# Swapping two of the small products of a split matmul, and drawing both score products of a block together, in a linear-attention and Mish kernel

## The chip, the cores and the metric

The kernel runs on one core of a Trainium2 chip. The metric is device time in microseconds (us) of one execution; lower is better. The median of three runs of the kernel before is 208.18 us (207.81 to 208.47).

## The reference, cut to what matters

```python
# retention: B=4, H=8, S=768, D=64
state = gamma[None, :, None, None] * state + einsum('bhd,bhe->bhde', k[:, :, t], v[:, :, t])
y[:, :, t] = scale * einsum('bhd,bhde->bhe', q[:, :, t], state)     # for every t
x = y.transpose(0, 2, 1, 3).reshape(B * S, H * D)                   # 3072 x 512
h = x @ w_in                                                        # 512 -> 2048
g = h * tanh(softplus(h))                                           # Mish
out = g @ w_out                                                     # 2048 -> 512
```

## The kernel before, in words

The 3072 tokens are 24 chunks of 128, grouped in 11 blocks: one of four chunks, then ten of two (256 tokens). A block goes through retention (scores, mask, outer product, state, y), then through the first product with Mish (`g1`), then through the second product (`g2`). TensorE ("PE") does all products in fp16. The retention work of the following block is woven by hand into the products of the current one: the schedule is manual, so every engine runs its instructions in the order in which the Python text issues them.

From block 3 (`SEVEN`) on, so in the last eight blocks, half of `g1` and all of `g2` are done as a 2x2 split with seven small products instead of eight, the sums and differences of the operands being made on VectorE ("DVE"). `g1_seven` writes the split half of `g1` into three PSUM tiles: `pb`, `px`, `pe`. `mm` is one small product, 8 matmuls of 128 columns. `px` is used four times: its contents after the first and after the third use are copied out by ScalarE ("ACT") with `snap` (L606, as `m1` and `u2`); `pe` is copied once (`m5`). `plus` (L616) is a DVE addition of a PSUM tile and such a copy, and gives `c11`, `c12`, `c22`; `mish_of` (L610) is the Mish of such a quarter on ACT. The other half of `g1` is done in four whole units, `plain(1,0)`, `plain(1,1)`, `plain(3,0)`, `plain(3,1)`: 8 matmuls of 256 columns each (L623) and one Mish on ACT (L627). A product that accumulates on a PSUM tile must wait until earlier readers of that tile are through.

Where `g1_seven` calls `step(name)`, the woven work of `steps_of` is issued. `scores(g)` (L371) makes the scores of chunk `g`: 8 matmuls with weights of 64 rows and 128 columns, into a tile of the pool `atps`, which has two buffers shared by the outer products `u_ps`, both score tiles and `y_ps`. `mask(g)` (L377) multiplies them by the causal mask on DVE. With `a = first[blk] + 4`, chunks `a - 2` and `a - 1` belong to the next block; the last block has no such work.

`sums_a(blk, half)` (L543 and L544, a pair of DVE operations) makes half of the operands `s1` and `s2` of the second product out of `g`. Half 0 needs the Mish of `c11`, `c12` and `c22`; half 1 needs the Mish of all four plain units. `seven` then does the second product: `mm(px, a(0,0))`, `mm(pb, a(0,1))`, `mm(px, s(2))` and so on (L688), 8 matmuls of 256 columns each. The third of these takes its weights from `s2`: its first four matmuls from half 0, its last four from half 1.

GpSimd ("POOL") casts the loaded q, k and v (L319, L324, L325) and finishes the states (L398). SyncE ("SP") issues loads, stores and the transposes of q and k by DMA (L331).

The end of `g1_seven`, around the change, reads:

```python
step("p6")
plain(1, 0)
mm(pe, s(4), b(1, 1));  c12 = plus(pe, u2)
mm(px, s(3), t(3));     c22 = plus(px, m5)
mish_of(0, 1, c12);     mish_of(1, 1, c22)
step("p7")              # stores, second state, sums_a half 0
plain(1, 1)
mm(px, a(1, 1), t(4));  mish_of(1, 0, px)
step("p4")              # stores, scores(a - 2), mask(a - 2)
plain(3, 0);  plain(3, 1)
step("end")             # sums_a half 1, scores(a - 1), casts, loads
```

Of the kernel before, what the change touches and what calls it, by code (L numbers as in the profile page):

```python
# [16 lines left out]
def kernel(  # L17
# [78 lines left out]
    for c in range(2):  # L96
        t = tri_first[c * HB:(c + 1) * HB]
# [367 lines left out]
    def win(s, f, bp):  # L465
        return wins[s, f // 2][:, bp, f % 2 * P:(f % 2 + 1) * P]
# [13 lines left out]
    def xt(blk, bp):  # L480
        return xts[0][:, :, bp] if blk == 0 else xts[blk][:, bp, :BLOCKS[blk] * C]
# [82 lines left out]
    def x_part(blk, i, j):  # L564
        n = NBP // 2
        return xts[blk][:, i * n:(i + 1) * n, j * P:(j + 1) * P]
# [10 lines left out]
    def g1_seven(blk, steps):  # L577
        n = NBP // 2
        gt = gtiles[blk, 0] = gp.tile([P, NFB, 2 * P], FP16, name="g", tag="g")
        for fb in range(NFB):  # L580
            gts[blk, fb] = gt[:, fb]
        pb, px, pe = [mmps.tile([P, FPS, P], FP32, name="h_ps", tag="mm") for _ in range(3)]

        def a(i, j):
            return lambda f, d: win(2 * i, f, j * n + d)

        def s(i):
            return lambda f, d: wsums[0][:, i - 1, d, f * P:(f + 1) * P]

        def b(i, j):  # L590
            return lambda d: x_part(blk, i, j)[:, d]

        def t(i):
            return lambda d: tsums[blk][:, i - 1, d]

        def mm(h_ps, w, x, first=False):
            for f in range(FPS):
                for d in range(n):
                    nc.tensor.matmul(  # L599
                        h_ps[:, f], w(f, d), x(d), start=first and f == 0 and d == 0,  # L600
                        stop=d == n - 1, skip_group_check=True)

        def snap(h_ps):
            x = hsnaps[0][:, nsnap[0] % 4].rearrange("p (f t) -> p f t", t=P)
            nsnap[0] += 1
            nc.scalar.copy(x, h_ps)  # L606
            return x

        def mish_of(i, j, h):
            nc.scalar.activation(  # L610
                gt[:, 2 * i * FPS:(2 * i + 1) * FPS, j * P:(j + 1) * P], h, AF.Mish,
                scale=inv_boost3)

        def plus(h_ps, x):
            h = hp.tile([P, FPS, P], FP32, name="hsum", tag="hsum", bufs=3)
            nc.vector.tensor_tensor(h, h_ps, x, op=ALU.add)  # L616
            return h

        def plain(s, half):
            h_ps = mmps.tile([P, 2, 2 * P], FP32, name="h_ps", tag="mm")  # L620
            for j in range(2):
                for bp in range(NBP):
                    nc.tensor.matmul(  # L623
                        h_ps[:, j], win(s, 2 * half + j, bp), xt(blk, bp),
                        start=bp == 0, stop=bp == NBP - 1)
            fb = s * FPS + 2 * half
            nc.scalar.activation(gt[:, fb:fb + 2], h_ps, AF.Mish, scale=inv_boost3)  # L627

        def step(name):
            for fn, *args in steps.get(name, ()):  # L630
                fn(*args)

        mm(px, a(0, 0), b(0, 0), True)
        m1 = snap(px)
        mm(pb, a(0, 1), b(1, 0), True)
        c11 = plus(pb, m1)
        step("p2")
        mm(pe, s(1), t(1), True)
        m5 = snap(pe)
        mm(px, s(2), t(2))  # L640
        u2 = snap(px)
        mish_of(0, 0, c11)
        step("p6")
        plain(1, 0)
        mm(pe, s(4), b(1, 1))
        c12 = plus(pe, u2)
        mm(px, s(3), t(3))
        c22 = plus(px, m5)
        mish_of(0, 1, c12)
        mish_of(1, 1, c22)  # L650
        step("p7")
        plain(1, 1)
        mm(px, a(1, 1), t(4))
        mish_of(1, 0, px)
        step("p4")
        plain(3, 0)
        plain(3, 1)
        step("end")

# [227 lines left out]
    def steps_of(blk):  # L887
        a, nb = first[blk] + 4, blk + 1
        ahead = nb < len(BLOCKS)

        def only(*work):
            return list(work) if ahead else []
        return {
            "p2": only((outer_next, nb), (state_next, nb, 0)),
            "p6": [(cast_to, a + 1), (next_chunk, a), (store_due, 1)],
            "p7": [(store_due, 2), *only((state_next, nb, 1)), (sums_a, blk, 0)],
            "p4": [(store_due, 3), *only((scores, a - 2), (mask, a - 2))],
            "end": [(sums_a, blk, 1), *only((scores, a - 1)),
                    (cast_to, a + 2), (next_chunk, a + 1)],
            "m2": only((mask, a - 1)),  # L900
            "m7": only((y_two, nb)),
            "m3": only((x_sums, nb)),
        }
# [13 lines left out]
    for blk in range(1, len(BLOCKS)):  # L917
        if blk >= SEVEN:
            steps = steps_of(blk)
            g1_seven(blk, steps)  # L920
            seven(blk, steps, blk + 1 == len(BLOCKS))
            continue
# [7 lines left out]
        for u in range(2 * n1):  # L930
# [3 lines left out]
            else:  # L934
                t, part = divmod(u - n1, 4)
# [43 lines left out]
```

## Time and profile before

| | |
|---|---|
| median of three runs | 208.18 us (207.81 to 208.47) |
| profiled execution | 207.9 us, of which the span of instructions is 206.0 us |
| granted TensorE clock | 1.0 |
| PE busy | 197.2 us (96% of the span) |
| DVE, ACT, POOL busy | 143.1, 98.3, 90.6 us |
| one of the last eight blocks | 15.2 to 15.5 us |

In the views of the profile a row is an engine, a line of the kernel, the operation, and the tiles written and read. Times run from the start of the span. The chain of waits follows the work that ended last back to what released it; the timeline merges instructions that follow each other, so that a merged PE row ends with the modelled end of its last matmul while the next row has already begun. The distance between the starts of two PE rows is the time that the first one takes from TensorE.

### The profile page before, as it was taken

The page shows a single profiled execution, that of the slowest core. Times are in us where ns is not written, and L with a number is a line of the kernel's source. Part 1 is how long each engine was busy: PE and PEld are TensorE (multiplying, and loading weights), DVE is VectorE, ACT ScalarE, POOL GpSimd, SP SyncE. Part 2 cuts the span into 40 slices and gives each one's busy share as a digit, 9 for nine tenths or more (in the row PEclk, how much of TensorE's full clock was granted, in tenths as well). Part 3 has the DMA queues.
Part 4 walks back from the last instruction along what each step waited for, and adds up shares of the span by engine and source line. Part 5 has one row for each costly group of instructions (what it writes and reads, how often), then busy time and mean ns, then how long its engine had stood idle before and what let it go on. Part 6 is the DMA issues. An engine that isn't in the chain of part 4 may idle for free.

```text
span 206.0 us, 5180 instructions
## 1 busy us (share of the span) xinstructions
PE 197.2 (96%) x2167; PEld 150.2 (73%) x2167; DVE 143.1 (69%) x234; ACT 98.3 (48%) x171; POOL 90.6 (44%) x83
## 2 busy tenths in 40 slices
PE   6788999999999999999999999999999999999993
PEld 2355444456855865988988988888888888888882
DVE  2796644169937986788897787686897687686542
ACT  2462763242611621653653653753753743843840
POOL 4162000519955760399182594598091693200000
PEclk9999999999999999999999999999999999999999
DMA  5999999998999999939998159959999062200202
GB/s 177 299 316 363 386 387 279 292 220 176 201 247 262 216 221 237 180 70 214 227 253 178 35 109 225 178 105 267 194 256 190 18 156 56 100 0 26 80 28 77
DMA packets 95896, 38.64 MB, mean 188 GB/s; under 512 B 82305, under 2 KB 89985, under 8 KB 95873
## 3 DMA queue, kind: packets, MB, share of 16 engines
q1 hardware_dynamic: 92608, 37.50, 80.3%
q10 hardware_dynamic: 3264, 0.82, 2.4%
q8 instruction: 17, 0.28, 0.5%
q14 instruction: 7, 0.05, 0.1%
HBM read 27.30 MB, written 6.29 MB: 163 GB/s over the span
## 4 chain that ended last, share of the span: by engine, by line
PE 83%; DVE 9%; ACT 2%; DMA 2%; issue 2%; DVEq 0%
PE o_ps L688 24%; PE h_ps L475 13%; PE o_ps L497 11%; PE h_ps L599 11%; PE h_ps L623 11%; DVE hsum L616 5%; PE at L371 3%; PE y_ps L414 2%; DMA qfirst<-in_q_dram 2%; PE y_ps L404 2%; PE u_ps L385 2%; DVE am L377 1%; PE h_ps L760 1%; ACT xt L460 1%; DVE qfirst L196 1%
## 5 line engine op out<-in xcount | busy, mean ns | idle before, releaser
L319 POOL TENSOR_TENSOR qk<-qf,qvs 128x512 f16<-128x512 f32 x20 | 22.5, 1127 | 28.4 <-DMA qf<-in_q_dram 26.4
L623 PE MATMUL h_ps<-xt,win 128*128 128x256 f16 x256 | 31.9, 273 | 0.0
L398 POOL TENSOR_TENSOR st<-su,gcm 128x512 f16<-128x512 f32 x9 | 11.9, 1321 | 41.7 <-DVE su L397 31.3
L497 PE MATMUL o_ps<-wout,g 128*128 128x512 f16 x128 | 30.1, 380 | 0.0
L324 POOL TENSOR_SCALAR qk<-kf 128x512 f16<-128x512 f32 x18 | 27.8, 1546 | 2.1 <-DMA kf<-in_k_dram 0.6
L377 DVE TENSOR_TENSOR am<-at,tri 128x1024 f16<-128x1024 f32 x20 | 24.1, 1214 | 4.6 <-PE at L371 4.6
L688 PEld LDWEIGHTS <-gsum 128*128 128x128 f16 x256 | 24.4, 98 | 3.6 <-DVE gsum L666 0.2
L475 PE MATMUL h_ps<-xt,win 128*128 128x256 f16 (+1 forms) x184 | 26.5, 305 | 0.3
L623 PEld LDWEIGHTS <-win 128*128 128x128 f16 x256 | 23.7, 98 | 3.1
L475 PEld LDWEIGHTS <-win 128*128 128x128 f16 x184 | 18.0, 98 | 9.0 <-issue 0.8
L491 ACT ACTIVATE g<-h_ps 128x512 f16<-128x512 f32 x32 | 19.0, 597 | 11.4 <-PE h_ps L475 10.0
L325 POOL TENSOR_TENSOR v<-vf,qvs 128x512 f16<-128x512 f32 x20 | 21.6, 1079 | 6.3 <-DMA vf<-in_v_dram 4.9
L460 ACT CAST xt<-y_ps 128x1024 f16<-128x1024 f32 x10 | 10.1, 1012 | 28.9 <-PE y_ps L414 21.6
L616 DVE TENSOR_TENSOR hsum<-h_ps,hsnap 128x512 f32<-128x512 f32 x24 | 15.8, 686 | 9.4 <-PE h_ps L599 8.2
L688 PE MATMUL o_ps<-tmat,gsum 128*128 128x256 f16 x192 | 22.3, 273 | 0.0
L627 ACT ACTIVATE g<-h_ps 128x512 f16<-128x512 f32 x32 | 19.0, 593 | 4.8 <-PE h_ps L623 4.8
L497 PEld LDWEIGHTS <-g 128*128 128x128 f16 x128 | 11.7, 98 | 13.0 <-issue 0.3
L606 ACT COPY hsnap<-h_ps 128x512 f32<-128x512 f32 x24 | 13.3, 588 | 15.6 <-PE h_ps L599 15.6
L688 PEld LDWEIGHTS <-g 128*128 128x128 f16 x192 | 18.2, 98 | 2.8
L694 ACT COPY snap<-o_ps 128x256 f32<-128x256 f32 x24 | 8.9, 372 | 20.3 <-PE o_ps L688 20.3
L702 DVE TENSOR_TENSOR osb<-o_ps,snap 128x256 f32<-128x256 f32 x24 | 10.1, 419 | 11.7 <-PE o_ps L688 9.0
L610 ACT ACTIVATE g<-hsum 128x512 f16<-128x512 f32 x24 | 15.0, 635 | 3.4 <-DVE hsum L616 3.4
(94 smaller groups left out, 291.0 us busy)
## 6 DMA issues: line engine op xcount, KB each, us to landing
kf<-in_k_dram SPq DMA_DIRECT2D x23, 256.0 KB, 5.1
vf<-in_v_dram SPq DMA_DIRECT2D x23, 256.0 KB, 5.1
out_dram<-osb SPq DMA_DIRECT2D x22, 256.0 KB, 3.8
qf<-in_q_dram SPq DMA_DIRECT2D x19, 256.0 KB, 4.0
wt<-in_moe_w_out_dram SPq DMA_DIRECT2D x3, 1024.0 KB, 8.9
wi<-in_moe_w_in_dram SPq DMA_DIRECT2D x4, 512.0 KB, 7.3
wi<-in_moe_w_in_dram SPq DMA_DIRECT2D x2, 1024.0 KB, 11.3
qfirst<-in_q_dram SPq DMA_DIRECT2D x2, 512.0 KB, 5.0
```

What stands on the lines that cost most here:

```text
L319: nc.gpsimd.tensor_tensor(q16, qf, qs.unsqueeze(2).broadcast_to((P, H, D)), op=ALU.mult)
L324: nc.gpsimd.tensor_scalar(k16, kf, BOOST, None, op0=ALU.mult)
L325: nc.gpsimd.tensor_tensor(v16, vf, vs.unsqueeze(2).broadcast_to((P, H, D)), op=ALU.mult)
L377: nc.vector.tensor_tensor(am, ats.pop(g), tri.unsqueeze(1).unsqueeze(1).broadcast_to((P, 2, HP, C)), op=ALU.mult)
L475: nc.tensor.matmul(h_ps[:, j], win(s, f, bp), xt(blk, bp), start=(bp == 0), stop=(bp == NBP - 1))
L491: nc.scalar.activation(gt, h_ps, AF.Mish, scale=inv_boost3)
L497: nc.tensor.matmul(o_ps, gts[blk, fb][:, t * P:(t + 1) * P], wouts[s][:, f, cols], start=(fb == 0), stop=(fb == NFB - 1))
L599: nc.tensor.matmul(h_ps[:, f], w(f, d), x(d), start=first and f == 0 and d == 0, stop=d == n - 1, skip_group_check=True)
L616: nc.vector.tensor_tensor(h, h_ps, x, op=ALU.add)
L623: nc.tensor.matmul(h_ps[:, j], win(s, 2 * half + j, bp), xt(blk, bp), start=bp == 0, stop=bp == NBP - 1)
L627: nc.scalar.activation(gt[:, fb:fb + 2], h_ps, AF.Mish, scale=inv_boost3)
L688: nc.tensor.matmul(o_ps, x(f), w(f), start=first and f == 0, stop=f == n - 1, skip_group_check=True)
```

## The change

Three things are reordered in `g1_seven`; no arithmetic is added or removed.

1. `mm(px, s(3), t(3))` with its addition `c22` goes ahead of `mm(pe, s(4), b(1, 1))` with its addition `c12`, and the Mish of `c22` ahead of that of `c12`.
2. `scores(a - 2)` moves from ahead of `plain(3, 0)` to behind it, and `scores(a - 1)` from behind `plain(3, 1)` to ahead of it; both now follow each other in a new step `h2`.
3. `mask(a - 2)` is issued in that step, behind both. On DVE it keeps its place in the order, between the two halves of `sums_a`.

```diff
         plain(1, 0)
+        mm(px, s(3), t(3))
+        c22 = plus(px, m5)
         mm(pe, s(4), b(1, 1))
         c12 = plus(pe, u2)
-        mm(px, s(3), t(3))
-        c22 = plus(px, m5)
+        mish_of(1, 1, c22)
         mish_of(0, 1, c12)
-        mish_of(1, 1, c22)
         step("p7")
         plain(1, 1)
         mm(px, a(1, 1), t(4))
         mish_of(1, 0, px)
         step("p4")
         plain(3, 0)
+        step("h2")
         plain(3, 1)
         step("end")
...
-            "p4": [(store_due, 3), *only((scores, a - 2), (mask, a - 2))],
-            "end": [(sums_a, blk, 1), *only((scores, a - 1)),
-                    (cast_to, a + 2), (next_chunk, a + 1)],
+            "p4": [(store_due, 3)],
+            "h2": only((scores, a - 2), (scores, a - 1), (mask, a - 2)),
+            "end": [(sums_a, blk, 1), (cast_to, a + 2), (next_chunk, a + 1)],
```

## The prediction

> **What bounds the kernel now.** I read the page first, for the engine that bounds.
>
> ```profile
> PE 197.2 (96%) x2167; PEld 150.2 (73%) x2167; DVE 143.1 (69%) x234; ACT 98.3 (48%) x171; POOL 90.6 (44%) x83
> ```
>
> TensorE is busy for 96% of the span at a granted clock of 1.0, so only idle time of PE or work taken from PE can shorten the kernel. The chain of waits, in order of time, shows where in a block the chain leaves PE. Columns: start us, length us, what. This is the end of the first product in the block that starts at 113.03.
>
> ```profile
> 114.54 0.89 PE h_ps L599 x16
> 115.43 0.87 PE h_ps L623 x8
> 116.31 0.46 PE h_ps L599 x8
> 116.81 0.04 issue
> 116.86 1.30 DVE hsum L616 x2
> 118.16 0.04 issue
> 118.20 0.61 PE h_ps L599 x8
> 118.80 0.33 PE at L371 x8
> 119.14 1.85 PE h_ps L623 x16
> 120.99 0.33 PE at L371 x8
> 121.32 4.47 PE o_ps L688 x40
> ```
>
> The two additions on DVE, `c12` then `c22`, stand on the chain: the last use of `px` (118.20) waits for `c22`, the second of them. The view of who waited for whom counts it, in us, times, longest:
>
> ```profile
> PEld L599 <- issue: 2.4, 8, 0.3
> ```
>
> The timeline around the same place, PE and then ACT:
>
> ```profile
> 115.27 1.04 PE L623 MATMUL h_ps<-xt,win 128*128 128x256 f16 x8
> 116.14 0.61 PE L599 MATMUL h_ps<-xt,wsum 128*128 128x128 f16 x8
> 117.03 1.04 PE L623 MATMUL h_ps<-xt,win 128*128 128x256 f16 x8
> ...
> 115.08 1.07 ACT L606 COPY hsnap<-h_ps 128x512 f32<-128x512 f32 x2 [0.81 <-PE h_ps L599]
> ```
>
> `plain(1,1)` starts at 117.03; the same eight matmuls of `plain(1,0)` took 116.14 - 115.27 = 0.87, so PE is free at 117.90 and idles 0.30 until 118.20. Eight blocks, 2.4 us.
>
> **Part 1, the swap.** It puts one wait in the place of another. The new one: `px` now comes directly behind `plain(1,0)`, and must wait for its copy `u2`, the second of the ACT pair, which ends at 115.08 + 1.07 = 116.15; with the 0.04 "issue" that the chain shows for a handover, `px` starts at 116.19 instead of 116.14: 0.05 lost. In the first of the eight blocks the copy ends 0.05 sooner and nothing is lost. The bounds are 0 and 0.10 a block; I take 0.05 because copy and PE stand in the same distance (0.88) in seven blocks. Queued behind this wait on PE are `pe`'s product and everything after it, so the 0.05 counts in full up to the next slack. The gain: the addition starts 116.86 - 116.14 = 0.72 behind its product, so at 116.91, takes 0.69 (group mean of L616 is 686 ns), and `px` is free at 117.65. PE gets there at 116.19 + 0.45 + 0.44 + 0.87 = 117.95. The old wait is gone with 0.30 to spare, and the last `px` product starts 0.25 earlier (0.30 in the first block). `c12` is now second on DVE and ends about 0.05 later than `c22` did; what follows on DVE and ACT (the state, `sums_a` half 0) waits for both additions in either order, so it moves by 0.05 only.
>
> **Part 2, the scores.** Per visit of 8 matmuls the starts show 0.33 (118.74 to 119.07, 120.92 to 121.25), and 0.09 to 0.10 ahead of it: the last `px` product needs 0.45 from 118.20, so 118.65, and the scores start at 118.74. Two visits are 0.85. Earlier in the run 16 such matmuls stand together:
>
> ```profile
> 59.79 0.62 PE L371 MATMUL at<-qkt 64*128 64x128 f16 x16
> 60.34 1.90 PE L497 MATMUL o_ps<-wout,g 128*128 128x512 f16 x8
> ```
>
> That is 0.55, with 0.09 ahead: 0.64 to 0.65. One visit saves 0.20 to 0.21, in seven blocks (the last has none). Costs that I set at nothing: the second score tile needs the buffer of `u_ps`, free when the state's first addition (118.06 + 0.68 = 118.74) is through, and PE needs it only at about 119.6; the transposes of q and k were issued 9 us or more earlier; `mask(a - 2)` can start at about 119.9 instead of 119.64 and takes 1.22, before DVE is wanted again at 121.6. DVE, ACT, POOL and SP keep their order, so no DMA passes another.
>
> **What this makes of a block.** Second product: before at 121.25; after at 117.95 + 0.45 + 0.87 + 0.65 + 0.87 = 120.79. That is 0.46 earlier in six blocks, 0.50 in the first, 0.24 in the last: 3.5 us if nothing else were late.
>
> **What is late next.** `plain(3,1)` doesn't move. Before it ended at 120.82, with one score visit behind it; after, both visits are ahead of it and it ends at 120.79. So its Mish and `sums_a` half 1 stay where they are, while the consumer, the third small product of `seven`, comes 0.46 earlier. The timeline, DVE, POOL and weight loads, shows how much room there was:
>
> ```profile
> 121.65 0.49 DVE L543 TENSOR_TENSOR gsum<-g 128x512 f16<-128x512 f16 x1 [0.79 <-ACT g L627]
> 121.82 1.22 POOL L319 TENSOR_TENSOR qk<-qf,qvs 128x512 f16<-128x512 f32 x1
> 122.17 1.15 DVE L544 TENSOR_TENSOR gsum<-gsum,g 128x512 f16<-128x512 f16 x1
> 123.38 0.10 PEld L688 LDWEIGHTS <-gsum 128*128 128x128 f16 x1
> ...
> 183.29 0.42 DVE L544 TENSOR_TENSOR gsum<-gsum,g 128x512 f16<-128x512 f16 x1
> ```
>
> L544 takes 0.42 at 183.29, where POOL is done, but 1.15 at 122.17, where POOL's two-input L319 runs until 123.04: DVE is held. It ends at 123.32, and the fifth weight load of the third product, due at 123.34 (one each 0.109), comes at 123.38: it already waits for DVE, within what PE tolerates. After the change it is due at 122.88 and comes at 123.36 to 123.38: 0.46 to 0.50 of idle PE, the whole gain of that block.
>
> [...]
>
> By block (due: new start of the second product + 2.09, from 123.34 - 121.25; ready: end of L544 + 0.055, from 123.32 to 123.38):
> - from 82.43: due 92.04, L544 ends 92.52: gain 0.50 eaten, 0.
> - from 97.80 and 143.73: L543 is queued behind the mask and half held by L324. In the first, due 105.55 + 2.09 = 107.64, ready 107.76 + 0.055 + 0.05: 0.2 lost, 0.26 left, each.
> - from 113.03 and 158.97: 0.
> - from 128.49: due 138.12, ready 138.17: 0.43 left.
> - from 174.43: L544 ends 183.71, due 184.06: all 0.46.
> - last: chain and consumer move together, 0.24.
>
> Sum: 0.52 + 0.43 + 0.46 + 0.24 = 1.65 us. The profiled execution is 207.9 (span 206.0 and 1.9 around it), so 206.25; the median of the runs is 208.18, 0.28 above that execution, so 206.5.
>
> **The rivals.**
> - The second pair is not held at the new places, or POOL shifts with DVE so that it slips in ahead: the whole 3.5, so 204.7. For it: L544's 0.42 where POOL is idle. Against: Mish, DVE and POOL keep their distances within 0.05, and three blocks hang on that pair today. [...]
> - The whole gain is eaten in all six blocks in which POOL works: 0.46 + 0.24 = 0.7 is left, so 207.5. Against it: the block from 128.49 shows only 0.05 missing.
> - Slower: the pair is held longer than today, by the new 0.05 shift of state and POOL. Mechanism: L543 runs its 0.49 and L544 then meets the start of a two-input POOL operation and takes 1.37, the worst row of it (150.00). In the block above it would end at 121.63 + 0.49 + 0.03 + 1.37 = 123.52, the load 0.70 behind its due time; less 0.46, that is 0.24 slower in six blocks, 1.44, less the 0.7 of the others: 208.9. With L543 held as well (0.93, its worst) 211.6. It decides once L544 ends past 123.3. For it: today's rows span 0.42 to 1.37; against it: no block's order on DVE or POOL changes.
> - The swap doesn't do what it says: the copy of `u2` comes late enough (0.3) to take the old wait's place. Then only the scores are gained, with the same cuts: 0.2 in four blocks, so 207.4. Against it: 0.05 in seven blocks.
>
> **How the numbers follow.** Forecast 206.5 with 0.64; no hold 204.7 with 0.12; all six eaten 207.5 with 0.11; slower 208.9 with 0.07; swap without effect 207.4 with 0.06. A measurement can tell about 0.3%, 0.62 us, from no change. So faster (below 207.56): 0.64 + 0.12, half of 0.11 and most of 0.06: 0.85; same 0.08; slower 0.07. The range from 205.0 to 207.7 holds the forecast with the new wait at its bounds (0.10 x 8 = 0.8 less, or 0.4 more), a hold that is gone in two of the three full blocks (1.0 more), and the cases at 207.4 and 207.5; it leaves out 0.12 below and 0.07 above.
>
> **What would show it.** Right: the idle PE time ahead of the last `px` product (2.4, 8 times) is gone, and the scores stand as one row of 16. The third product of `seven` now waits for L544 in the blocks from 82, 113 and 159, 0.4 to 0.5 each, less in those from 98 and 144; block lengths stay near 15.4 there and fall to about 14.8 in the seventh. Wrong: that wait is absent (then near 204.7) or stands in the seventh block too; or the idle time moved ahead of `px`'s third use.

## The result and the profile after

The changed kernel takes 206.37 us (median of 4 runs, 206.14 to 206.52) against 208.0 us (207.78 to 208.47) on the same chip: ratio 0.9918, 95% interval 0.9896 to 0.9939. The forecast was 206.5. The profiled execution is 206.36 us with a span of 204.4.

The engine that bounds, on the page of the changed kernel:

```profile
PE 195.9 (96%) x2167; PEld 149.9 (73%) x2167; DVE 142.3 (70%) x234; ACT 97.5 (48%) x171; POOL 91.7 (45%) x83
```

The chain of waits in order of time (start us, length us, what), for the same block as before, which here starts at 112.91:

```profile
115.31 0.87 PE h_ps L623 x8
116.18 0.95 PE h_ps L599 x16
117.13 0.87 PE h_ps L623 x8
118.00 0.45 PE h_ps L599 x8
118.45 0.87 PE h_ps L623 x8
119.33 0.55 PE at L371 x16
119.88 0.99 PE h_ps L623 x8
120.87 0.02 issue
120.89 0.61 ACT g L627
121.50 0.02 issue
121.52 0.56 DVE gsum L543
122.08 0.02 issue
122.10 1.16 DVE gsum L544
123.26 0.05 issue
123.31 2.36 PE o_ps L689 x20
```

Up to 120.87 the chain no longer leaves PE: the two DVE additions are off it, and the scores are one row of 16. Then it leaves PE at a new place: Mish of `plain(3,1)`, L543, L544, and only then the third small product (L689 is the old L688). The view of who waited for whom, the same lines of it:

```profile
PEld L689 <- DVE gsum L544: 2.1, 5, 0.6
PE o_ps L689 <- DVE gsum L544: 0.8, 3, 0.3
```

The old entry of 2.4 us for L599 is gone; weight loads of five blocks now wait for L544, and in three of them PE then idles for 0.43 to 0.44. The timeline there, DVE, POOL, weight loads and PE:

```profile
122.10 1.15 DVE L544 TENSOR_TENSOR gsum<-gsum,g 128x512 f16<-128x512 f16 x1
121.75 1.22 POOL L319 TENSOR_TENSOR qk<-qf,qvs 128x512 f16<-128x512 f32 x1
123.30 0.22 PEld L689 LDWEIGHTS <-gsum 128*128 128x128 f16 x3 [0.55 <-DVE gsum L544]
122.44 0.60 PE L689 MATMUL o_ps<-tmat,gsum 128*128 128x256 f16 x4
123.31 2.36 PE L689 MATMUL o_ps<-tmat,gsum 128*128 128x256 f16 x20 [0.27 <-DVE gsum L544]
```

L544 is held as long as before (1.15), while L319 runs. The weight load that was 0.04 late now starts 0.55 after the end of the one in front of it. From one PE row to the next, four matmuls, it is 0.87 where they need 0.44, so PE idles for 0.43.

Lengths of the eight blocks, each from the first PE row of its first small product to that of the next block (the last to the end of the span, within 0.03), in us:

| block, by its start before | 82 | 98 | 113 | 128 | 144 | 159 | 174 | 190 | sum |
|---|---|---|---|---|---|---|---|---|---|
| before | 15.37 | 15.24 | 15.46 | 15.24 | 15.24 | 15.46 | 15.24 | 16.34 | 123.6 |
| changed | 15.22 | 14.92 | 15.46 | 14.79 | 14.93 | 15.45 | 14.79 | 16.08 | 121.6 |
| gain | 0.15 | 0.32 | 0 | 0.45 | 0.31 | 0.01 | 0.45 | 0.26 | 1.95 |
| predicted | 0 | 0.26 | 0 | 0.43 | 0.26 | 0 | 0.46 | 0.24 | 1.65 |

The spans differ by 1.6 and not by 1.95 because the stage ahead of these blocks, which the change doesn't touch, took 82.77 instead of 82.43 in this execution; over all profiled executions of this study it lies between 81.9 and 82.8. The table is therefore the sharper measure, and below the runs are read by it too.

### The profile page after: what moved, and what is told of

The parts are those of the page before. It is cut to its first block, busy times and chain, and to the rows that moved or that the text cites. A ratio compares the mean times of both kernels' runs of the same rounds, so it can differ in the third digit from the quotient of the medians.

```text
span 204.4 us, 5174 instructions
## 1 busy us (share of the span) xinstructions
PE 195.9 (96%) x2167; PEld 149.9 (73%) x2167; DVE 142.3 (70%) x234; ACT 97.5 (48%) x171; POOL 91.7 (45%) x83
## 4 chain that ended last, share of the span: by engine, by line
PE 76%; DMA 8%; POOL 4%; DVE 4%; ACT 2%; SPq 2%; issue 2%; POOLq 0%; DVEq 0%
PE o_ps L689 21%; PE h_ps L623 14%; PE h_ps L599 12%; PE o_ps L497 10%; PE h_ps L475 6%; DMA qkt<-qk 3%; DMA qf<-in_q_dram 3%; PE at L371 2%; DMA qfirst<-in_q_dram 2%; POOL qk L324 2%; PE y_ps L414 2%; PE u_ps L385 2%; PE y_ps L404 2%; DVE gsum L544 1%; POOL v L325 1%
## 5 line engine op out<-in xcount | busy, mean ns | idle before, releaser
L319 POOL TENSOR_TENSOR qk<-qf,qvs 128x512 f16<-128x512 f32 x20 | 23.0, 1150 | 29.1 <-DMA qf<-in_q_dram 29.1
L623 PE MATMUL h_ps<-xt,win 128*128 128x256 f16 x256 | 33.1, 273 | 0.0
L398 POOL TENSOR_TENSOR st<-su,gcm 128x512 f16<-128x512 f32 x9 | 11.9, 1319 | 38.1 <-DVE su L397 38.1
L324 POOL TENSOR_SCALAR qk<-kf 128x512 f16<-128x512 f32 x18 | 27.8, 1543 | 1.5
L689 PEld LDWEIGHTS <-gsum 128*128 128x128 f16 x256 | 24.0, 98 | 5.5 <-DVE gsum L544 2.1
L325 POOL TENSOR_TENSOR v<-vf,qvs 128x512 f16<-128x512 f32 x20 | 22.2, 1111 | 7.8 <-DMA vf<-in_v_dram 6.3
L689 PE MATMUL o_ps<-tmat,gsum 128*128 128x256 f16 x192 | 23.1, 273 | 0.8 <-DVE gsum L544 0.8
L497 PEld LDWEIGHTS <-g 128*128 128x128 f16 x128 | 11.7, 98 | 12.9 <-issue 0.3
L689 PEld LDWEIGHTS <-g 128*128 128x128 f16 x192 | 18.8, 98 | 2.2
```

The costliest lines, as they stand in the source:

```text
L319: nc.gpsimd.tensor_tensor(q16, qf, qs.unsqueeze(2).broadcast_to((P, H, D)), op=ALU.mult)
L324: nc.gpsimd.tensor_scalar(k16, kf, BOOST, None, op0=ALU.mult)
L325: nc.gpsimd.tensor_tensor(v16, vf, vs.unsqueeze(2).broadcast_to((P, H, D)), op=ALU.mult)
L497: nc.tensor.matmul(o_ps, gts[blk, fb][:, t * P:(t + 1) * P], wouts[s][:, f, cols], start=(fb == 0), stop=(fb == NFB - 1))
L623: nc.tensor.matmul(h_ps[:, j], win(s, 2 * half + j, bp), xt(blk, bp), start=bp == 0, stop=bp == NBP - 1)
L689: nc.tensor.matmul(o_ps, x(f), w(f), start=first and f == 0, stop=f == n - 1, skip_group_check=True)
```

## The experiments

Theory, called the hand-back: each part of the change gives PE its full time, and the second pair of `sums_a` in a block (half 1: L543 and L544), held by POOL, takes some of it back. Rival: the parts are simply worth less than computed, and nothing is handed back. The median of the kernel before was 207.54 beside the first four runs and 207.77 beside the last four.

**e1, the swap alone**

```diff
         plain(1, 0)
+        mm(px, s(3), t(3))
+        c22 = plus(px, m5)
         mm(pe, s(4), b(1, 1))
         c12 = plus(pe, u2)
-        mm(px, s(3), t(3))
-        c22 = plus(px, m5)
+        mish_of(1, 1, c22)
         mish_of(0, 1, c12)
-        mish_of(1, 1, c22)
```

> Theory (hand-back): only the two products of px and pe are swapped, the scores stay where they were before. PE reaches the last px product 0.25 us earlier and all that follows, plain(3,1) and its Mish included, moves with it. Where POOL works beside the second pair of sums_a (blocks from about 82, 113 and 159) the end of L544 stays and the 0.25 is lost again; in the other five blocks 0.25 each is kept: about 1.2 us less than before, near 206.8. In the trace the idle time ahead of the last px product (2.4 us, 8 times) is gone. Rival (parts add up, nothing is handed back): each part of the change brings about half of its 1.6 us, so 207.2, and no weight load of L688 waits for L544.

Measured: 206.39, ratio 0.9942 (0.993 to 0.9955). Blocks: 15.22, 15.01, 15.46, 15.01, 15.01, 15.46, 15.01, 16.08; sum 122.2, so 1.3 less than before, and 1.15 less by the medians, against 1.2 expected by the theory and 0.8 by the rival. The five blocks keep 0.23 to 0.26, and 113 and 159 keep nothing. The first block, expected at nothing, is 0.15 shorter, as it is in the changed kernel. In the view of who waited for whom stands:

```profile
PEld L688 <- DVE gsum L544: 1.0, 3, 0.4
```

This wait did not exist in that view before. The swap takes away 0.29 and puts 0.06 ahead of `px`'s third use, as computed. The medians alone part the two only narrowly (the rival's 0.8 would be a ratio of 0.996, and the interval ends at 0.9955); the two blocks that keep nothing and the new wait decide, for the hand-back.

**e2, the scores alone**

```diff
         plain(3, 0)
+        step("h2")
         plain(3, 1)
...
-            "p4": [(store_due, 3), *only((scores, a - 2), (mask, a - 2))],
-            "end": [(sums_a, blk, 1), *only((scores, a - 1)),
-                    (cast_to, a + 2), (next_chunk, a + 1)],
+            "p4": [(store_due, 3)],
+            "h2": only((scores, a - 2), (scores, a - 1), (mask, a - 2)),
+            "end": [(sums_a, blk, 1), (cast_to, a + 2), (next_chunk, a + 1)],
```

> Theory (hand-back): only the scores are drawn together behind plain(3,0), the products keep their order, so the idle 0.30 us ahead of the last px product stays. PE saves 0.21 a block, but plain(3,1) now ends 0.22 later than before while the second product starts 0.21 earlier. In the two blocks from about 113 and 159 L543 then falls behind the two-input L319 of POOL and L544 behind the start of L324, some 0.9 late: 0.7 lost in each. The four blocks from 98, 128, 144 and 174 keep 0.21. In sum about 0.6 slower, near 208.6. Rival (parts add up, nothing is handed back): 207.2.

Measured: 207.85, ratio 1.0006 (0.9996 to 1.0016): nothing gained. Blocks: 15.22, 15.03, 15.97, 15.03, 15.03, 15.98, 15.03, 16.32; sum 123.6, as before. Four blocks win their 0.21, and 113 and 159 lose 0.52 each. The timeline of the block from about 112, DVE and then PE:

```profile
121.09 1.26 DVE L543 TENSOR_TENSOR gsum<-g 128x512 f16<-128x512 f16 x1 [0.60 <-ACT g L627]
123.16 1.05 PE L689 MATMUL o_ps<-tmat,gsum 128*128 128x256 f16 x8 [0.55 <-DVE gsum L544]
```

The mechanism is the one expected: moved 0.22 later, L543 itself (0.49 before, 1.26 here) falls behind L319, which POOL runs from 121.04 to 122.08 here. The size is not: I had 0.7 lost in each of the two, and nothing gained in the first block, which won 0.15. So 0 and not 0.6; the rival's 207.2 is excluded all the same. So the gain of this part depends on the other part, which keeps `plain(3,1)` where it was.

**e3 and e4, s(1) ahead of s(2), with the change and without**

```diff
-        mm(px, s(2), t(2))
-        u2 = snap(px)
-        sums_c(blk)
         mm(pe, s(1), t(1), True)
         m5 = snap(pe)
+        sums_c(blk)
+        mm(px, s(2), t(2))
+        u2 = snap(px)
         mm(px, s(3), t(3))
```

> The changed kernel, and in the second product the small product with s(1) goes ahead of the one with s(2), so that s2, which L544 makes, is wanted 0.87 us later. Theory (hand-back): the waits of weight loads for L544 (2.1 us, 5 times, and 0.8 us at the matmul) go. Blocks from 98, 128, 144 and 174 keep all their 0.46, the last its 0.24; in those from 113 and 159 the later DVE work (L663, L667) is late next and leaves about 0.2 each; from 82 about 0.15. About 2.6 less than before, near 205.5. Rival (parts are just smaller than computed): no change against the changed kernel, 206.4.

> Control: the kernel before, with s(1) ahead of s(2) in the second product. There the weight load was within 0.05 us of its due time, so by the theory of the hand-back nothing is to be gained: 208.0, within 0.2. If the order of s(1) and s(2) is worth something by itself (for another reason than the wait for L544), it shows here as in the run with the changed kernel, near 207.1.

Measured: e3 209.35, ratio 1.0088 (1.0075 to 1.0101); e4 212.71, ratio 1.0255 (1.0239 to 1.0272). Both far from any figure expected. The waits of e3:

```profile
PEld L689 <- issue: 5.0, 8, 0.7
PE o_ps L689 <- ACT snap L695: 3.5, 7, 0.5
```

No wait for L544 is left, so that part holds; but I had overlooked that `px` is used again directly behind: `s(3)` now follows `s(2)` on the same tile and must wait for the ACT copy of it, 0.5 in that view. By the block lengths it costs 0.68 (in e4 the blocks from 98 and 113 take 15.92 and 16.14, before 15.24 and 15.46). It is the swap's own new wait, there 0.06 because a plain unit of 0.87 lies in between, and here with nothing in between.

Compared with the kernel before, neither run measures the hand-back. Compared with each other they do: both carry the new wait, they differ by the change alone, POOL does all its casts, and no weight load waits for L544 in either. e3 is 3.4 us below e4 (by the medians, and by block sums of 125.4 against 128.9), and each of the six blocks from 98 to 174 is 0.44 to 0.45 shorter. Where nobody waits for the second pair, the change brings its full time; without that reordering it brings 1.6 by the medians and 1.95 by the blocks.

**e5 and e6, POOL without the casts, before and changed**

```diff
         qf, kf, vf = loaded.pop(g)
+        if g > 12:
+            cast[g] = cast[12]
+            return
```

> The kernel before, without the casts of the chunks 13 to 23 on POOL: they use the cast tiles of chunk 12, so that part of the computation is left out. POOL then runs only the states (L398) beside the last eight blocks. Theory (hand-back through POOL): L543 and L544 of the second pair fall to 0.42 each in the blocks from about 98 on, but nobody on PE was waiting for them before the change, so the time stays: 207.5 on the chip of the runs e1 to e4, within 0.3. Rival (the pair is long for another reason than POOL): the pair keeps its 0.7 to 1.2 in the blocks from 113 and 159.

> The changed kernel with the same casts left out. Theory (hand-back through POOL): the pair is short, no weight load waits for L544 in the blocks without casts, and the change now brings what PE's own order gives: the second product starts 0.43 earlier in each of the blocks from 98 to 174 and 0.23 in the last, 0.15 in the first: near 3.0 less than the run e5, against 1.6 to 1.9 with the casts. Rival (the gain is lost elsewhere): e6 stays 1.6 to 1.9 below e5.

From chunk 13 on both kernels use the cast tiles of chunk 12, so part of the computation is left out. Measured: e5 207.54, ratio 1.0001 (0.999 to 1.0012); e6 204.38, ratio 0.9837 (0.9821 to 0.9854). Without the casts the change brings 3.2 us by the medians, with them 1.6. Blocks of e6: 14.76, 14.79, 15.02, 14.79, 14.79, 15.02, 14.79, 16.11, sum 120.1, against 123.45 in e5: 3.4. The second pair in the block that starts at 113 in the kernel before, timeline of e6 (DVE; L546 and L547 are the old L543 and L544):

```profile
120.82 0.41 DVE L546 TENSOR_TENSOR gsum<-g 128x512 f16<-128x512 f16 x1
121.27 0.42 DVE L547 TENSOR_TENSOR gsum<-gsum,g 128x512 f16<-128x512 f16 x1
```

No entry of the waits names L547 any more. Both halves of the theory are shown: the pair is long because of POOL's casts, and on the kernel before nobody waited for that (e5), while after the change it costs nearly half of the gain (3.4 against 1.95 by blocks).

**e7 and e8, other work for PE in the gap**

All of the computation stays. e7 draws the half of `y` that uses the past state ahead of the third small product; e8 also moves one DVE addition behind the sums `s4`.

```diff
 e7
-            "m2": only((mask, a - 1)),
-            "m7": only((y_two, nb)),
+            "m2": only((mask, a - 1), (y_past, nb)),
+            "m7": only((y_rest, nb)),
 e8, on top
         sums_b(blk)
-        done(0, 0, pb, m1)
...
         sums_c(blk)
+        done(0, 0, pb, m1)
         mm(pe, s(1), t(1), True)
```

`y_past` and `y_rest` are the two halves of `y_two`, cut between `past` and `present`.

> The changed kernel, all of its computation; only the half of y that takes the past state (L404 before, 4 or 8 matmuls, 0.31 to 0.45 us) is drawn ahead of the third small product of the second product, so that s2 is wanted that much later and PE does needed work in the gap. Theory (hand-back): nearly all waits for L544 go; in the blocks from 113 and 159 the next late thing is the last DVE sum (s4, by the line after sums_c, ends 11.2 after the first plain unit, wanted at 10.9), which leaves 0.1 of 0.43 there. Sum 0.45 + 4 x 0.43 + 2 x 0.1 + 0.23 = 2.6 less than before, ratio 0.9875. Rival (the parts are only smaller than computed): as the changed kernel, ratio 0.992.

> As e7, and the first DVE addition into the output (done(0,0), 0.34 us to the next start) goes behind the sums s4, so that s4 and the mask of the second chunk are 0.34 sooner. Theory (hand-back): s4 is ready at 10.86 and wanted at 10.93 in the blocks from 113 and 159, so these keep most of their 0.43 too: about 3.2 less than before, ratio 0.985. Rival (something else than the DVE sums holds these two blocks): as e7.

Measured: e7 204.69, ratio 0.9856 (0.9839 to 0.9873); e8 204.51, ratio 0.985 (0.9834 to 0.9866). Their block sums, 121.1 and 120.4, are 2.5 and 3.2 below the kernel before, where 2.6 and about 3.2 were expected. Blocks of e7: 15.36, 14.79, 15.23, 14.79, 14.79, 15.23, 14.79, 16.07; of e8: 14.76, 14.79, 15.17, 14.79, 14.79, 15.17, 14.79, 16.10. What PE's weight loads still wait for, in e7 and in e8 (L700 is the old L688, L678 the sum `s4`):

```profile
PEld L700 <- DVE gsum L678: 1.3, 3, 0.7
```

```profile
PEld L700 <- DVE gsum L678: 0.5, 2, 0.2
```

L544 is gone from both. What is late next is `s4`, as expected, in the blocks from 113 and 159 and, in e7, in the first. In e8 these two blocks keep 0.29 of 0.43 and not most of it: `s4` takes 0.95 against 0.68 in e7, because it now starts 0.34 sooner (10.17 instead of 10.51 behind `plain(1,0)`), while POOL's two-input L325 still runs:

```profile
123.84 1.04 POOL L325 TENSOR_TENSOR v<-vf,qvs 128x512 f16<-128x512 f32 x1
124.48 0.95 DVE L678 TENSOR_TENSOR gsum<-g,gsum 128x1024 f16<-128x1024 f16 x1
```

By time e8 can't be told from e7; most of what separates their block sums lies in the first block, where L678 took 1.46 in e7. Either beats the changed kernel (0.9918): the intervals don't overlap.

## Why the prediction was right, point by point

- **The idle 2.4 us.** Gone from the waits in all eight blocks. The new wait for the copy `u2` was put at 0.05 and measures 0.06 (the distance from `plain(1,0)` to the next row is 0.93 instead of 0.87); the first block has none, as said.
- **The scores.** One row of 16, 0.55, as in the earlier row of 16 on which the prediction built.
- **The second product's start.** Counted from `plain(1,0)` it moved from 5.98 to 5.55 in six blocks, 0.43 instead of the 0.46 predicted. The rest is rounding: the new wait is 0.06 and not 0.05, and a plain unit takes 0.875, which I had as 0.87 three times.
- **What is late next.** L544 ended 8.05 behind `plain(1,0)` before and 8.11 after in the block from 113: it moved by no more than the new wait, and PE idles 0.43 there, 0.43 in 159 and 0.44 in 82, which is the whole gain in the first two and all but 0.05 in 82. In 98 and 144 the idle time is 0.12 where I had 0.2, so these kept 0.32 and 0.31 instead of 0.26. The blocks from 128 and 174 keep all.
- **The one term that was wrong** is the first block, 0 instead of 0.15, of which 0.05 is that remainder. The other 0.10 has another source. Before, a later DVE sum, L666, took 1.46, and PE waited 0.10 for it; after the change the same sum (L667) took 0.68. I had read the 0.10 as fixed. It depends on where POOL stands: before, L319 began 0.13 ahead of that sum; after, it waited for its load and began 0.25 behind it:

```profile
94.39 1.04 POOL L319 TENSOR_TENSOR qk<-qf,qvs 128x512 f16<-128x512 f32 x1
94.52 1.46 DVE L666 TENSOR_TENSOR gsum<-g,gsum 128x1024 f16<-128x1024 f16 x1
...
94.86 0.68 DVE L667 TENSOR_TENSOR gsum<-g,gsum 128x1024 f16<-128x1024 f16 x1
95.11 1.33 POOL L319 TENSOR_TENSOR qk<-qf,qvs 128x512 f16<-128x512 f32 x1 [0.52 <-DMA qf<-in_q_dram]
```

In e4, with the first product as before, the sum also took 0.67, and in e7, on the changed kernel, the 1.46 is back and the block is 15.36 long. So it is not shown that this 0.10 comes from the change.

- **Where luck helped.** The mechanism held block by block, but the blocks gained 1.95 and not 1.65. That the profiled execution still took 206.36, where 206.25 was forecast, is because the stage ahead of the blocks was 0.34 longer in it. In the range, the new wait at its upper bound is counted as 0.8 us more; 0.4 of that is in the forecast already, so 0.4 was right.
- **The rivals.** The time without hold, 204.7, is what the casts on POOL deny: e6, without them, took 204.4, and in the block from 113 the second sum of the pair took 1.15 with the casts (L544) and 0.42 without (L547 in e6). The slower case came to its turning point in the blocks from 113 and 159 (L544 at 8.11, these blocks at 15.46 and 15.45) and in none beyond it; only in e2 does the pair come late enough to cost 0.5 in two blocks. The case of all six blocks eaten failed at 98, 128 and 144; the case of the swap without effect at e1, which brings 1.2 us.

## What to carry to other kernels

When an engine is busy for 96% of the span, a gain there is only kept as far as the next input is early (here 1.95 us by the blocks, against 3.4 without the casts): look up, for every kind of block, how far the following operands lie ahead of their due time (here a weight load that was already 0.04 late told it). Two edits need not add up: by the block sums the scores alone brought nothing, the swap alone 1.3 us, both 1.95, because the swap makes up for the delay that moving the scores puts ahead of `plain(3,1)`, whose result is due next. Once such an input is late, moving work that doesn't need it into the gap was worth nearly as much here as making the input faster: the eight blocks took 121.1 in e7 and 120.4 in e8, against 120.1 in e6 and 121.6 in the changed kernel.

## What the runs showed of the hardware that was not expected

- A fp16 sum of two 128x512 tensors on DVE takes 0.42 alone (L544 at 183.29, before), 0.71 to 0.82 when it begins 0.07 to 0.23 behind the start of POOL's one-input L324 (before: L543 at 106.49 takes 0.82, L544 at 137.41 takes 0.71), and up to 1.38 when it meets a two-input operation of POOL (L544 beside L398: 1.37 at 150.00 before, 1.38 at 149.49 in the changed kernel). Where it began under a running two-input operation, it ended 0.27 to 0.28 after that operation did: L544 at 123.32 after L319 at 123.04 and at 151.37 after L398 at 151.09 (before), L543 at 122.35 after L319 at 122.08 (e2). Moving a sum by 0.2 or 0.3 changed which operation it met: L543 took 1.26 in e2 against 0.49 before, and the 128x1024 sum `s4` 0.95 in e8 against 0.68 in e7. So its time here is not a property of the instruction that can be carried over to a new place.
- Executions of kernels that are the same up to there reach the first changed block between 81.9 us (e1) and 82.8 us (the changed kernel). Differences of span below 1 us are better read from the blocks behind it.
